# Constant fills and the first pair's products on VectorE, and the first batch's maximum of V twelve steps later, in a fused attention and two-layer feed-forward kernel

## The chip, the cores and the metric

The kernel runs on one core of a Trainium2 chip. The metric is the device time of one launch in microseconds (us); lower is better. Three runs of the kernel before took 1356.93, 1356.93 and 1362.55 us, so its median is 1356.93 us. PE is TensorE (matmuls), PEld its weight loads, DVE is VectorE, ACT is ScalarE, POOL is GpSimd, and SP is the engine whose queue issues all DMAs here.

## What is computed

The inputs are 4 batches of 12 heads, 448 rows and 64 columns. Attention is followed by a gated feed-forward layer and a second one with a cosine:

```python
q_n, k_n = rmsnorm(q, g_q), rmsnorm(k, g_k)
scores = scale * np.matmul(q_n, k_n.transpose(0, 1, 3, 2))
attn = softmax(scores)                       # rows, with their maximum taken off
x = np.matmul(attn, v)                       # heads are put side by side: 1792 x 768
g = x @ moe_w_gate
x = (g / (1 + exp(-g)) * (x @ moe_w_val)) @ moe_w_out
h = x @ moe2_w_in
out = (h * np.cos(h)) @ moe2_w_out
```

## The kernel before

**Pairs.** Two heads form a pair, so each batch has six pairs; those of batch 0 are numbered 0 to 5 here. Numbers are carried as a high and a low half in float16, so that most matmuls come in threes.

**Stages.** First the six pairs of batch 0 go through attention alone. Then the feed-forward pieces of batch b run (`mm_piece`, L1002 to L1004), with the attention of batch b+1 between them, and then the second layer. The weights are 64-bit-wide in memory: each load (768 KB, L821) is turned into 32-bit words by three DVE instructions (L841 to L843, one conversion), squared by ACT for a scale (L861), and split.

**A pair of batch 0**, in the order of its data:

- `p_load` loads its q and k (L281, L284), `c_v` its V in five DMAs (L606 to L609).
- `p_sq` squares (ACT, L311) and sums (DVE, L312); `p_pow` raises to the power -1/2 on POOL (L321) and, on DVE, multiplies k by the gains (L325).
- `p_mul` multiplies k (DVE, L363) and q (POOL, L364) by that root. `p_khi` and `p_qhi` copy the high halves (ACT, L378, L392), and `p_klo` and `p_qlo` subtract them to leave the low halves (POOL, L384, L398). Which engine does which is said by sets of letters, one set for each batch (`CF`, read by `cfg`): "qm", "kl" and "ql" put q's product and the two low halves on POOL.
- `c_T` transposes the halves by a DMA (L614) into a tile T. T has three buffers in this stage, so the transposition of pair 3 waits until pair 0's last matmul on T is done, that of pair 4 for pair 1, that of pair 5 for pair 2.
- `c_copy` moves parts of T (DVE L621 and L622, ACT L623). `c_s` makes seven score tiles only for their maxima (PE L634, DVE L635).
- `c_row` turns the maxima into a row (DVE L641 and L642, PE L646, ACT L647). `c_st` makes the transposed scores with that row taken off (PE L664) and their exponentials (ACT L667).
- `c_av` multiplies by V (PE L677), into two PSUM banks t and u that have one buffer each. `c_x` divides by the sums (ACT L683 and L684, DVE L685, a reciprocal, and two results at L690), using `vs2`. Only then are t and u free for the next pair.

**The maximum of V.** V is scaled by a power of two from the largest magnitude in its batch. `v_max(b)` loads V of the batch in two halves into the raw buffers that the weights also use (L333, 672 KB each), reduces each on DVE (L334), joins the partitions by a matmul (L337), makes the scales with five small DVE instructions (L339 to L343), and spreads them by a second matmul (L346) and a copy (L347). For batch 0 it also makes `vs2` (L349), which `c_x` needs.

**Constants.** `c_const(i)` fills, for each of three buffers C, the lower 64 partitions with zeros (L587) and two single rows with -2^14 (L589), and fills two other tiles, all on POOL.

**What sets the order.** The program emits steps n = -32 to 52 for batch 0 (`LEAD` is 33). In each step it emits pieces of several pairs. `v_max(0)` is emitted ahead of step `VM0 - LEAD`, `v_max(1)` after step `VM1` = 2. A scheduling layer then puts each engine's instructions in a fixed order, by its own estimate of times. On the chip each engine works through its own list strictly in that order, and SP its DMAs: an instruction that waits holds up everything behind it.

The raw buffers are three, taken in turn. The PSUM banks of the first feed-forward matmuls are those that `c_av` and `c_st` used, so that L1002 starts when `c_x` of pair 5 has read them.

Of the kernel before, what the change touches and what calls it, by code (L numbers as in the profile page):

```python
# [24 lines left out]
FD = 1  # L25
FH = 1
YS = (3, 2)
VM0 = 22
VM1 = 2
CAV = 1  # L30
CXX = 8
# [9 lines left out]
         26: [("split", 1), ("conv", 3), ("load", 5)]}  # L41
UNITS = ((0, 2, 4, 5), (0, 2, 4, 6), (0, 2, 4, 6), (0, 2, 4, 6))
SCH = ((1, 0), (0, 0), (1, 1))
OFF = ({'load': -25,
  'vload': -18,
  'sqk': -17,
# [94 lines left out]
def kernel(ctx: ExitStack, tc, q, k, v, g_q, g_k, w_gate, w_val, w_out, w2_in, w2_out, out):  # L141
    nc = tc.nc
# [12 lines left out]
    HP = P // 2  # L155
# [116 lines left out]
        return src[b, 2 * p:2 * p + 2].rearrange("h (q t) d -> (h q) t d", t=NS)  # L272

    def cfg(g):
        return CFS[g // NP]

    def p_load(g):
# [9 lines left out]
    def p_vload(g):  # L287
        rv = pool("rv", g).tile([P, 2, NS, D], F32, tag="rv", name="rv")
        b, p = divmod(g, NP)
        vs = v[b, 2 * p:2 * p + 2].rearrange("h (q t) d -> q h (t d)", t=NS)  # L290
        rv2 = rv.rearrange("p h t d -> p h (t d)")
        nc.sync.dma_start(rv2[:HP], vs)
        nc.sync.dma_start(rv2[HP:, :, :S - D], vs[:, :, D:])
        if g < NP:
            pass
        elif "vw" in cfg(g):
            nc.vector.tensor_copy(rv[HP:, :, NS - 1], rv[:HP, :, 0])
        else:
            nc.sync.dma_start(rv2[HP:, :, S - D:], vs[:, :, :D])
        prep[g]["rv"] = rv  # L300

    def p_sq(g, j):
        pg = prep[g]
        if j == 1:
            pg["ss"] = pools["sm"].tile([P, 2 * NS], F32, tag="ss", name="ss")
        sq = pool("sq", g, 2 * g + j).tile([P, S], F32, tag="sq", name="sq")
        src = pg["rqk"][:, j].rearrange("p g d -> p (g d)")
        if ("sq", "sk")[j] in cfg(g):
            nc.gpsimd.tensor_tensor(sq, src, src, op=ALU.mult)
        else:  # L310
            nc.scalar.activation(sq, src, AF.Square)  # L311
        nc.vector.tensor_reduce(  # L312
            pg["ss"][:, NS * j:NS * j + NS], sq.rearrange("p (g d) -> p g d", d=D), axis=AX.X, op=ALU.add
        )

    def p_pow(g):
        pg = prep[g]
        ss = pg["ss"]
        nc.vector.tensor_scalar(ss, ss, 1.0 / (D * PQ * PQ), 1e-6 / (PQ * PQ), op0=ALU.mult, op1=ALU.add)  # L319
        ri = pools["sm"].tile([P, 2, NS], F32, tag="ri", name="ri")  # L320
        nc.gpsimd.tensor_tensor(ri.rearrange("p a b -> p (a b)"), ss, half[:, :2 * NS], op=ALU.pow)  # L321
        pg["ri"] = ri
        if "kf" in cfg(g):
            k3 = pg["rqk"][:, 1]
            nc.vector.tensor_tensor(k3, k3, gk.unsqueeze(1).to_broadcast([P, NS, D]), op=ALU.mult)  # L325

    def v_max(b):
        half_n = H * S * D // P // 2
        src = v[b].rearrange("h s d -> (h s d)").rearrange("(p x) -> p x", p=P)
        vm = nm_p.tile([P, 4], F32, tag="nm", name="vm")  # L330
        for i in range(2):
            t = rot("raw").tile([P, 6 * 256], I32, tag="raw", name="raw")
            nc.sync.dma_start(t[:, :half_n].bitcast(F32), src[:, i * half_n:(i + 1) * half_n])  # L333
            nc.vector.tensor_reduce(vm[:, i:i + 1], t[:, :half_n].bitcast(F32), axis=AX.X, op=ALU.max, apply_absolute_value=True)  # L334
        nc.vector.tensor_max(vm[:, 2:3], vm[:, 0:1], vm[:, 1:2])
        ps = bank(ps_s, "s")
        nc.tensor.matmul(ps[:1, :P], vm[:, 2:3], ident, start=True, stop=True)  # L337
        row = nm_p.tile([1, 4], F32, tag="nm", name="vrow")
        nc.vector.tensor_reduce(row[:, 0:1], ps[:1, :P], axis=AX.X, op=ALU.max)  # L339
        nc.vector.tensor_scalar(row[:, 1:2], row[:, 0:1], 1e-30, None, op0=ALU.max)  # L340
        nc.vector.tensor_scalar(row[:, 1:2].bitcast(I32), row[:, 1:2].bitcast(I32), 0x7F800000, None, op0=ALU.bitwise_and)
        nc.vector.reciprocal(row[:, 2:3], row[:, 1:2])
        nc.vector.tensor_scalar(row[:, 2:3], row[:, 2:3], PV, None, op0=ALU.mult)  # L343
        nc.vector.tensor_scalar(row[:, 3:4], row[:, 1:2], 1.0 / (2.0 * PV), None, op0=ALU.mult)
        ps = bank(ps_s, "s")
        nc.tensor.matmul(ps[:, :2], full[:1], row[:, 2:4], start=True, stop=True)  # L346
        nc.vector.tensor_copy(vsc[:, 2 * b:2 * b + 2], ps[:, :2])  # L347
        if b == 0:
            nc.vector.tensor_scalar(vs2, vsc[:, 0:1], 2.0, None, op0=ALU.mult)  # L349
# [231 lines left out]
    def ctile(nm, shape, dt, g=None):  # L581
        return c_p.tile(shape, dt, tag="c" + nm, name="c" + nm, bufs=COL[nm])

    def c_const(i):

        C = ctile("C", [P, NS, P], F16)
        nc.gpsimd.memset(C[HP:], 0.0)  # L587
        for r in (HP, HP + 32):
            nc.gpsimd.memset(C[r:r + 1], -(2.0 ** 14))  # L589
        W = ctile("w", [P, NS, HP], F16)  # L590
        nc.gpsimd.memset(W, 0.0)
        if i < 2:
            V = ctile("V", [P, 4, 2, P], F32)
            nc.gpsimd.memset(V[:, :, 0, HP:], 1.0)
            nc.gpsimd.memset(V[:, :, 1, :HP], 1.0)
            colv[i] = V
        colc[i] = (C, W)
# [122 lines left out]
    def ph(g):  # L720
        return PH[g if g < NP else NP - 1 + g // NP]

    LEAD = -min(OFF[ph(g)][nm] + NS * g - CSH for g in range(NP) for nm, f in PREP)

    def s_prep(n):
        for nm, f in PREP:
            for g in range(NPAIR):
                if NS * g + OFF[ph(g)][nm] - (CSH if g < NP else 0) == n:
                    if g < NP and nm in ("vhi", "vlo"):
# [448 lines left out]
    for i in range(3):  # L1178
        c_const(i)
    step(-LEAD, 0)  # L1180
    for n in range(1 - LEAD, NB + NTAIL):
        if n == VM0 - LEAD:
            v_max(0)
# [22 lines left out]
    for b in range(B):  # L1206
        sched = {}
        if b + 1 < B:
            nst = NB + NTAIL
            q0, q1 = SCH[b][0], per - SCH[b][1]  # L1210
            wt = [1 if q0 <= u < q1 else 0 for u in range(per)]
# [136 lines left out]
```

## Time and profile before

| | us |
|---|---|
| median of three runs | 1356.93 |
| the profiled execution's own time | 1358.27 |
| its span, first to last instruction | 1356.5 |
| PE busy | 1199.2 (88%) |
| DVE busy | 883.3 (65%) |
| ACT busy | 684.4 (50%) |
| POOL busy | 474.5 (35%) |
| first matmul on a tile T | 37.59 |
| first feed-forward matmul (L1002) | 158.36 |

The profiled execution spends 1.77 us outside its span, and is 1.34 us above the median. In the rows of the next section but one, a row of a timeline says when a group of instructions started, how long it took from its first start to its last end, engine, line, operation, what it writes and reads, the shape, how many were merged (x3), and in brackets how long the engine had stood idle ahead of it and what it waited for. Neighbouring instructions of an engine overlap a little: one reduction of 448 elements takes 0.61 us, but the next starts some 0.53 us after it.

### The profile page before, as it was taken

To read this page: it belongs to the slowest core of one execution; us is meant where nothing else is said; L and a number is where in the kernel's file an instruction comes from. 1 tells how busy PE (TensorE), PEld (TensorE's weight loads), DVE (VectorE), ACT (ScalarE), POOL (GpSimd) and SP (SyncE) were. 2 spreads that over 40 slices of the span, in tenths; PEclk is the share of its full clock that TensorE was granted. 3 is DMA by queue.
4 is the path that set the end of the run, shared out by engine and by line. 5 is a ranking of instruction groups with operands and counts; after the bars stand their busy time and mean duration, and the time that the engine had idled before them with its cause. 6 is when DMAs were issued, how large, how long until landed. Compare 5 with 4: busy or idle time off the path is not lost.

```text
span 1356.5 us, 18241 instructions
## 1 busy us (share of the span) xinstructions
PE 1199.2 (88%) x6454; PEld 676.3 (50%) x6454; DVE 883.3 (65%) x1556; ACT 684.4 (50%) x1318; POOL 474.5 (35%) x351
## 2 busy tenths in 40 slices
PE   0588787878799978999999998979998999999998
PEld 0233343334574435854458655955444555666665
DVE  7868968999967787647763399477889875100000
ACT  2567577775435556445664365456767776100000
POOL 8621335555733456623554013503323332000000
PEclk9889798788899999999999999989999999999999
DMA  7535559987999976789867688641113222633121
GB/s 239 142 82 143 175 149 241 242 215 216 244 327 276 219 170 157 194 231 203 187 131 191 217 305 292 233 160 48 47 47 129 82 82 70 212 110 100 58 88 41
DMA packets 255195, 227.02 MB, mean 167 GB/s; under 512 B 177280, under 2 KB 205952, under 8 KB 255104
## 3 DMA queue, kind: packets, MB, share of 16 engines
q1 hardware_dynamic: 255104, 225.86, 59.3%
q8 instruction: 50, 0.82, 0.3%
q14 instruction: 41, 0.34, 0.1%
HBM read 147.13 MB, written 38.77 MB: 137 GB/s over the span
## 4 chain that ended last, share of the span: by engine, by line
PE 45%; DVE 19%; DMA 6%; ACT 4%; issue 3%; POOL 1%; SPq 0%; DVEq 0%; ACTq 0%; POOLq 0%
PE mm L1002 9%; PE mm L1003 8%; PE mm L1004 8%; PE mm L1015 7%; PE s L1015 7%; DMA T<-h 3%; PE t L1015 2%; DVE w L842 2%; DVE w L843 2%; PE t L555 2%; DVE w L841 2%; DMA PT<-p 2%; DVE tmp L1140 1%; PE s L444 1%; DVE sm L453 1%
## 5 line engine op out<-in xcount | busy, mean ns | idle before, releaser
L1002 PE MATMUL mm<-xy,wp 128*128 128x448 f16 x960 | 347.4, 363 | 35.9 <-DVE tmp L1144 12.2
L1003 PE MATMUL mm<-xy,wp 128*128 128x448 f16 x960 | 347.9, 362 | 0.0
L1004 PE MATMUL mm<-xy,wp 128*128 128x448 f16 x960 | 342.7, 362 | 2.2 <-DVE wp L874 2.1
L1015 PEld LDWEIGHTS <-g 128*128 128x128 f16 x1344 | 131.5, 98 | 87.2
L1002 PEld LDWEIGHTS <-wp 128*128 128x128 f16 x960 | 97.9, 102 | 120.9 <-issue 25.9
L1003 PEld LDWEIGHTS <-wp 128*128 128x128 f16 x960 | 96.3, 100 | 108.9 <-issue 33.5
L1004 PEld LDWEIGHTS <-wp 128*128 128x128 f16 x960 | 94.9, 100 | 98.5 <-issue 10.3
L1149 POOL TENSOR_TENSOR g<-tmp,g 128x448 f16<-128x448 f32 x64 | 73.7, 1165 | 188.3 <-ACT g L1148 188.3
L496 POOL TENSOR_TENSOR p<-pr,p 128x448 f16<-128x448 f32 x72 | 89.9, 1252 | 140.9 <-ACT p L487 122.2
L943 POOL TENSOR_TENSOR wp<-w,wp 128x768 fp32r<-128x768 f32 x48 | 96.3, 2010 | 79.7 <-ACT wp L942 50.2
L463 ACT ACTIVATE pr<-s,sm,esc 128x448 f32<-128x448 f32 x126 | 90.2, 718 | 60.0 <-DVE sm L457 56.8
L1002 PE MATMUL mm<-g,wp 128*128 128x448 f32 x288 | 108.6, 378 | 0.0
L1003 PE MATMUL mm<-g,wp 128*128 128x448 f32 x288 | 107.2, 372 | 0.0
L1004 PE MATMUL mm<-g,wp 128*128 128x448 f32 x288 | 106.7, 371 | 0.2 <-POOL wp L943 0.2
L1050 POOL TENSOR_TENSOR g<-tmp,g 128x448 fp32r<-128x448 f32 x48 | 63.8, 1343 | 108.7 <-ACT g L1049 108.5
L1015 PE MATMUL s<-wp,g 128*128 128x384 f16 x576 | 100.1, 326 | 0.0
L1015 PE MATMUL mm<-wp,g 128*128 128x384 f16 x576 | 99.1, 326 | 0.0
L453 DVE TENSOR_REDUCE sm<-s 128x1 f32<-128x448 f32 x126 | 75.5, 615 | 20.2 <-PE s L444 19.9
L487 ACT ACTIVATE p<-pr 128x448 f16<-128x448 f32 x126 | 70.0, 570 | 28.1 <-DMA PT<-p 27.1
L321 POOL TENSOR_TENSOR ri<-ss,half 128x14 f32<-128x14 f32 x24 | 64.5, 2692 | 47.1 <-DVE ss L319 39.3
L1160 ACT ACTIVATE tmp<-mm,osc 128x384 f32<-128x384 f32 x8 | 4.7, 581 | 148.6 <-PE mm L1015 147.8
L842 DVE SCALAR_TENSOR_TENSOR w<-raw,w 128x768 int32<-128x768 int32 x68 | 76.6, 1138 | 0.8
(170 smaller groups left out, 2078.0 us busy)
## 6 DMA issues: line engine op xcount, KB each, us to landing
raw<-in_moe_w_out_dram SPq DMA_DIRECT2D x28, 768.0 KB, 5.2
wp<-scr_gate SPq DMA_DIRECT2D x36, 384.0 KB, 4.4
wp<-scr_val SPq DMA_DIRECT2D x36, 384.0 KB, 4.7
w<-scr_out SPq DMA_DIRECT2D x36, 384.0 KB, 4.0
raw<-in_moe_w_in_dram SPq DMA_DIRECT2D x16, 768.0 KB, 4.7
raw<-in_moe_w_gate_dram SPq DMA_DIRECT2D x12, 768.0 KB, 5.5
raw<-in_moe_w_val_dram SPq DMA_DIRECT2D x12, 768.0 KB, 5.0
wp<-scr_out SPq DMA_DIRECT2D x24, 384.0 KB, 3.0
```

Source lines behind the costliest of these rows:

```text
L321: nc.gpsimd.tensor_tensor(ri.rearrange("p a b -> p (a b)"), ss, half[:, :2 * NS], op=ALU.pow)
L453: nc.vector.tensor_reduce(sm[:, 0, t:t + 1], slot[n][:, :S], axis=AX.X, op=ALU.max)
L463: nc.scalar.activation(e, slot.pop(n)[:, :S], AF.Exp, bias=sm[:, 1, t:t + 1], scale=esc, accum_out=sm[:, 2, t:t + 1],)
L487: nc.scalar.activation(hi, slot[n], AF.Copy)
L496: eng.tensor_sub(p16[:, t - t0, 1], slot.pop(n), p16[:, t - t0, 0])
L842: nc.vector.scalar_tensor_tensor(wi, hi, -0x40000000, wi, op0=ALU.bitwise_and, op1=ALU.bitwise_or)
L943: nc.gpsimd.tensor_sub(wl, w32, wh.bitcast(F32))
L1002: nc.tensor.matmul(ps[f][:, :S], wh[:, s], x[:, 0], start=(first and i == 0), stop=False)
L1003: nc.tensor.matmul(ps[f][:, :S], wh[:, s], x[:, 1], start=False, stop=False)
L1004: nc.tensor.matmul(ps[f][:, :S], wl[:, s], x[:, 0], start=False, stop=(last and i == n - 1))
L1015: nc.tensor.matmul(ps[:, :CO], x[:, a, p0:p0 + P], rhs, start=st, stop=sp)
L1149: nc.gpsimd.tensor_sub(x[:, 1], r, x[:, 0])
```

## The change

Three things are changed. `VM0` goes from 22 to 34, so that `v_max(0)` is emitted ahead of step 1 in place of step -11, just ahead of `v_max(1)`. The fills of C (three of zeros, six single rows) go from POOL to DVE. Pair 0 gets a set of its own, without "qm", "kl" and "ql": `p_mul` then multiplies q and k in one DVE instruction (L369 of the changed kernel), and both low halves are DVE subtractions. "kf" and "xl" stay as they were.

```diff
-VM0 = 22
+VM0 = 34
...
+FIRST = {'kf', 'xl'}
...
     def cfg(g):
+        if g == 0:
+            return FIRST
         return CFS[g // NP]
...
-        nc.gpsimd.memset(C[HP:], 0.0)
+        nc.vector.memset(C[HP:], 0.0)
         for r in (HP, HP + 32):
-            nc.gpsimd.memset(C[r:r + 1], -(2.0 ** 14))
+            nc.vector.memset(C[r:r + 1], -(2.0 ** 14))
```

Lines of the changed kernel are one higher from L44 on and three higher from L277 on. Three places in the engines' lists follow.

DVE around pair 0's product (rqk_285 and h16_312 or h16_313 are pair 0's, vm_357 and vm_470 are `v_max(0)`'s), before:

```order
L334 TENSOR_REDUCE vm_357<-raw_358 128x1
L334 TENSOR_REDUCE vm_357<-raw_361 128x1
L335 TENSOR_TENSOR vm_357<-vm_357 128x1
L339 TENSOR_REDUCE vrow_367<-s_365 1x1
L363 TENSOR_TENSOR rqk_285<-rqk_285,ri_308 128x448
L340 TENSOR_SCALAR vrow_367<-vrow_367 1x1
L341 TENSOR_SCALAR vrow_367<-vrow_367 1x1
L342 RECIPROCAL vrow_367<-vrow_367 1x1
```

and of the change:

```order
L337 TENSOR_REDUCE vm_470<-raw_471 128x1
L322 TENSOR_SCALAR ss_337<-ss_337 128x14
L369 TENSOR_TENSOR rqk_285<-rqk_285,ri_308 128x896
L337 TENSOR_REDUCE vm_470<-raw_474 128x1
L366 TENSOR_TENSOR rqk_303<-rqk_303,ri_329 128x448
L387 TENSOR_TENSOR h16_312<-rqk_285,h16_312 128x7x64
L401 TENSOR_TENSOR h16_312<-rqk_285,h16_312 128x7x64
L338 TENSOR_TENSOR vm_470<-vm_470 128x1
L366 TENSOR_TENSOR rqk_323<-rqk_323,ri_357 128x448
L844 TENSOR_SCALAR w32_735<-raw_579 128x768
```

Pair 0's product has moved ahead of the second half's reduction, and the low halves stand behind that reduction.

SP's list at the first loads of V (raw tiles are for the maximum, cV_267 is pair 0's V and cV_276 pair 1's), before:

```order
L284 DMA rqk_324<-in_q_dram 128x448
L333 DMA raw_358<-in_v_dram 128x1344
L333 DMA raw_361<-in_v_dram 128x1344
L606 DMA cV_267<-in_v_dram 64x4x64
...
L609 DMA cV_267<-in_v_dram 64x64
L606 DMA cV_276<-in_v_dram 64x4x64
```

and of the change:

```order
L287 DMA rqk_323<-in_q_dram 128x448
L609 DMA cV_267<-in_v_dram 64x4x64
...
L612 DMA cV_267<-in_v_dram 64x64
L336 DMA raw_471<-in_v_dram 128x1344
L336 DMA raw_474<-in_v_dram 128x1344
L609 DMA cV_276<-in_v_dram 64x4x64
```

The two halves for the maximum now stand behind the five loads of pair 0's V.

DVE between the rows of pair 0 (cw_265) and of pair 1 (cw_274), before:

```order
L641 TENSOR_SCALAR cw_265<-sm_386 128x7
...
L363 TENSOR_TENSOR rqk_521<-rqk_521,ri_694 128x448
L319 TENSOR_SCALAR ss_1081<-ss_1081 128x14
L339 TENSOR_REDUCE vrow_540<-s_538 1x1
...
L347 COPY vsc_101<-s_547 128x2
L635 TENSOR_REDUCE sm_448<-s_555 128x1
L635 TENSOR_REDUCE sm_574<-s_575 128x1
L641 TENSOR_SCALAR cw_274<-sm_448 128x7
```

and of the change (vm_529 is `v_max(1)`'s, vrow_480 `v_max(0)`'s and vrow_539 `v_max(1)`'s, w32_810 and w32_885 are the second and third conversion, T_663 is pair 3's, cr_644 pair 0's sums):

```order
L644 TENSOR_SCALAR cw_265<-sm_364 128x7
...
L337 TENSOR_REDUCE vm_529<-raw_530 128x1
L337 TENSOR_REDUCE vm_529<-raw_533 128x1
...
L844 TENSOR_SCALAR w32_810<-raw_581 128x768
...
L844 TENSOR_SCALAR w32_885<-raw_583 128x768
...
L624 COPY cB_679<-T_663 64x896
...
L688 RECIPROCAL cr_644<-cr_644 128x448
L343 TENSOR_SCALAR vrow_539<-vrow_539 1x1
L693 SCALAR_TENSOR_TENSOR tmp_649<-t_512,vs2_102,cr_644 64x448
...
L350 COPY vsc_101<-s_546 128x2
L638 TENSOR_REDUCE sm_426<-s_554 128x1
...
L644 TENSOR_SCALAR cw_274<-sm_426 128x7
```

Between the two rows now also stand the two reductions of `v_max(1)`, two weight conversions, pair 3's `c_copy` and pair 0's `c_x`; before, those reductions and conversions stood ahead of pair 0's first score maximum, and the `c_copy` and `c_x` behind pair 1's row.

## Rows read from the trace of the kernel before

**Rows 1.** Windows: stretch, length, PE, PEld, DVE, ACT, POOL busy, PEclk, DMA share, GB/s.

```profile
0.00:22.80 22.80, 1.17 (x4) 0.61 (x4) 12.89 (x35) 5.21 (x8) 21.36 (x34) 1.00 0.59 187
...
61.20:147.80 86.60, 73.72 (x285) 28.34 (x285) 66.66 (x107) 57.20 (x104) 18.36 (x14) 0.90 0.46 119
147.80:158.40 10.60, 1.16 (x9) 0.84 (x6) 10.52 (x13) 5.42 (x14) 7.96 (x5) 0.61 0.50 126
```

**Rows 2.** Timeline of the first 28 us, all engines.

```profile
1.27 0.84 POOL L587 MEMSET cC<- 64x896 f16 x1
...
7.37 0.90 SPq L333 DMA_DIRECT2D raw<-in_v_dram  x2
...
10.15 3.50 POOL L589 MEMSET cC<- 1x896 f16 x4
...
12.28 0.62 SPq L609 DMA_DIRECT2D cV<-in_v_dram  x1
...
13.74 7.72 POOL L321 TENSOR_TENSOR ri<-ss,half 128x14 f32<-128x14 f32 x3
...
16.70 1.55 DVE L334 TENSOR_REDUCE vm<-raw 128x1 f32<-128x1344 f32 x1 [1.02 <-DMA raw<-in_v_dram]
...
19.43 0.60 DVE L363 TENSOR_TENSOR rqk<-rqk,ri 128x448 f32<-128x448 f32 x1
...
21.57 1.27 DVE L363 TENSOR_TENSOR rqk<-rqk,ri 128x448 f32<-128x448 f32 x1
...
27.90 3.36 SPq L614 DMA_TRANSPOSE T<-h  x1
```

**Rows 3.** The raw tiles of the first 60 us: from issue to landing.

```profile
DMA to landing us min/median/max: 4.1/6.1/8.8
```

**Rows 4.** The transpositions of L614: from issue to landing.

```profile
DMA to landing us min/median/max: 4.0/4.2/6.2
```

**Rows 5.** Timeline of DVE from 22 to 76 us.

```profile
22.80 3.21 DVE L334 TENSOR_REDUCE vm<-raw 128x1 f32<-128x1344 f32 x2
...
30.97 0.55 DVE L841 TENSOR_SCALAR w<-raw 128x768 int32<-128x768 int32 x1
...
33.43 0.55 DVE L841 TENSOR_SCALAR w<-raw 128x768 int32<-128x768 int32 x1
...
36.42 1.11 DVE L622 COPY T<-T 64x896 f16<-64x896 f16 x1
...
49.88 0.17 DVE L641 TENSOR_SCALAR cw<-sm 128x7 f16<-128x7 f32 x1
...
61.15 0.94 DVE L641 TENSOR_SCALAR cw<-sm 128x7 f16<-128x7 f32 x1
...
66.97 0.39 DVE L621 COPY cB<-T 64x896 f16<-64x896 f16 x1 [1.75 <-DMA T<-h]
...
70.02 2.95 DVE L685 RECIPROCAL cr<-cr 128x448 f32<-128x448 f32 x1 [0.27 <-ACT cr L684]
...
75.12 0.69 DVE L690 SCALAR_TENSOR_TENSOR tmp<-u,vs,cr 64x448 f32<-64x448 f32 x1
```

**Rows 6.** Timeline of PE from 65 to 159 us.

```profile
65.45 0.41 PE L646 MATMUL s<-id,cw 128*64 128x128 f16 x4
...
68.49 0.58 PE L634 MATMUL s<-T 128*64 128x448 f16 x2 [2.27 <-DVE sm L635]
...
71.54 1.30 PE L664 MATMUL c<-cB,cC 128*128 128x448 f16 x3
...
93.93 3.47 PE L677 MATMUL t<-pr,cV 128*128 128x448 f32 x8
...
158.36 0.56 PE L1002 MATMUL mm<-xy,wp 128*128 128x448 f16 x1 [5.22 <-DVE tmp L690]
```

**Rows 7.** Timeline of SP's queue: the transpositions of pairs 3 and 4.

```profile
61.53 2.16 SPq L614 DMA_TRANSPOSE T<-h  x1
...
76.08 1.55 SPq L614 DMA_TRANSPOSE T<-h  x1
```

## The prediction

> **What bounds the kernel now.** I read the windows by stage first, because the change touches only the first stage, then the timeline of each engine there. Up to 22.8 us nothing is bound by work: DVE is busy for 12.89 us, PE for 1.17, and POOL for 21.36 [rows 1]. The reader should see POOL's queue in it: six row fills end at 13.65, and only then the three roots start, at 13.74 [rows 2]. DVE meanwhile stands at the second half of V, which lands at 16.70, and pair 0's product waits behind it until 19.43 [rows 2]. Its first transposition goes out at 27.90 [rows 2], and DVE has both copies done at 36.42 + 1.11 = 37.5 [rows 5]. From there on it is a chain of pairs: PE is busy for 73.7 of 86.6 us between 61.2 and 147.8, DVE for 66.7 [rows 1]. Neither is full; two loops tie them. Transpositions 3 and 4 go out when `c_st` of pairs 0 and 1 is done, at 61.53 and 76.08 [rows 7], and pair g+1 may multiply by V only when `c_x` of pair g has emptied t and u. The stage ends on DVE: busy for 10.52 of the last 10.6 us [rows 1], and L1002 starts when the last result of `c_x` is out, at 158.36 [rows 6].
>
> **Fills.** POOL loses 3 x 0.84 + 6 x 0.87 = 7.7 us [rows 2]. Its first root then starts when the sums are there, 2 to 3 us before 13.74. On DVE nothing of before shows such a fill. The bounds are nothing and POOL's own price, 7.7 us; I take the latter, the only row of the same shape. Five of nine stand ahead of the gains' arithmetic, where DVE waits for a load; four behind it cost 3.4 us, before the sums. DVE has 9.9 idle us in this window [rows 1], so either end is hidden. The Trainium skill, page "VectorE: DVE Perf Modes", section "Zero memsets can be issued as uint32 (trn2)", gives one cycle for each element of a fill whatever its type; by that the nine would take an estimated 7.0 us, and no run here shows it.
>
> **The head start.** Pair 0's product no longer waits for the V maximum's small instructions, but its low halves stand behind the reduction of V's second half, and V's halves now stand behind five loads of pair 0's V. Those take SP from 8.27 to 12.90, so the halves go out 4.6 us later, at 12 to 12.8 [rows 2]. Landing takes 4.1 to 8.8 us [rows 3]; the middle, 6.1, puts the second half at 18.9. Behind it stand its reduction, 1.55, and three operations at some 0.53 each (DVE's step between such instructions), so 22 to 22.5; with one hand-over from ACT I take 23, between 21 and 25. That is 4.9 us ahead of 27.90. The transposition lands 4.0 to 6.2 us later [rows 4]; I take 5.8, near the longest, since a weight load goes out just ahead of it. DVE has two instructions of that load's conversion ahead of `c_copy` and one within it, and is done at some 31.4, not 37.5. **Head start: 6.1 us.** Up to pair 0's row DVE's list then has the same instructions as before, 49.88 - 37.5 = 12.4 us [rows 5], so that the row comes at 43.8.
>
> **What it is paid with.** Between the rows of pairs 0 and 1 passed 61.15 - 49.88 = 11.3 us [rows 5]. Now the list has there as well: the two reductions of V of batch 1, 3.2; two conversions, each 33.43 - 30.97 = 2.46; pair 0's `c_x`, a reciprocal of 2.95 and two results of 0.7; and pair 3's two copies, 0.8 [rows 5]. Together 13.3 us. The second conversion's load can go out only when the first of the reductions has freed its buffer, near 50.5, and lands 4.1 us later at the least [rows 3], when DVE has been there for a microsecond; I add 1.5. Pair 1's row is then at 43.8 + 11.3 + 13.3 + 1.5 = 70, not 61.15. These are instructions that DVE did before under the wait for the first transposition; that cover is gone, and PE is queued behind them, since the second matmul of `v_max(1)` stands ahead of pair 1's last scores and waits for DVE's list to have passed pair 0's results.
>
> **How much comes back.** Before, PE had pair 1's row at 65.45 but began its `c_st` at 71.54, having waited for pair 3's copies (2.27 us of wait at 68.49) [rows 6], because transposition 3 went out at 61.53 and its copy began at 66.97 [rows 5, 7]. Now transposition 3 goes out near 54, when pair 0's `c_st` is done, and its copies lie in the list above. So PE goes from the row to `c_st` in some 3.6 us, at 73.6: 2.1 later than before. That `c_st` took 76.08 - 71.54 = 4.5 us [rows 6, 7]. Now four of pair 1's products with V stand within it, at 3.47 / 4 = 0.87 each [rows 6], and two more score tiles: some 9 us, and transposition 4 at 82.6, 6.5 late. From it to pair 2's products with V passed 93.93 - 76.08 = 17.9 us [rows 6, 7], half a pair's products (3.5) of which are done already: 97.0 in place of 93.93. **Net: 3 us late.** From there PE's list is the same as before up to L1002, and takes the same 64.4 us [rows 6]. DVE is full in the last 10.6 us [rows 1], so some of the lateness may vanish in PE's wait there; I leave it at 3, with nothing and 6.5 (transposition 4's own lateness) as ends. Where batch 1 lies between the feed-forward pieces, the lists differ in places until about a third of PE's instructions are through, and not after. I count nothing for it, and 4 us either way for the range, about what one displaced transposition costs [rows 4].
>
> **A rule against the change.** Pair 0's DVE product and subtractions, which read two tiles, now run beside POOL's roots. A DVE product took 0.60 us beside the roots at 19.43 and 1.27 beside a POOL product at 21.57 [rows 2]: the roots did not hold it, the product did. The Trainium skill, page "SBUF — State Buffer", section "The single rule", says that a DVE instruction with two SBUF inputs and a GpSimd instruction that reads SBUF exclude each other for a whole instruction. By that rule a root too could hold DVE; the trace agrees for the POOL product and not for the roots.
>
> **The sum.** The profiled execution took 1358.27 us; plus 3 is 1361.3. It lies 1.34 above the median of the three runs, so on the median's scale 1356.9 + 3 = 1360.
>
> **Rivals.**
> (1) The head start is kept. For it: in the 86.6 us of pairs DVE has 20 idle us [rows 1], and `c_x` of pair 0, done at 75.8 before [rows 5], is now done near 67, so t and u are free when pair 1 wants them. Against it: one list, in order. It decides by pair 1's row: ahead of 66 us, PE reaches pair 1's `c_st` ahead of 71.5 and the chain keeps 4 to 6 us. At 6.1 us the time is 1351. Chance 0.26.
> (2) The loop doesn't close again: products of pair 1 that are placed within `c_st` wait for their exponentials, so nothing of a pair's products is saved, and the 17.9 us count in full. Pair 2's come at 82.6 + 17.9 = 100.5, 6.5 late; with the bound for the later lists 1360 to 1367, middle 1363.5 to 1364. It decides from a fourth transposition later than 82 us. Slower than before. Chance 0.20.
> (3) The head start fails: pair 0's DVE instructions wait for a root of 7.72 / 3 = 2.6 us [rows 2]. Transposition 0 at 25.6 and everything 2.6 later than forecast: 1362.6. Chance 0.06; this is what the rule above would do, by the trace's own price.
> The forecast has the rest, 0.48.
>
> **Range and chances.** 0.5% is 6.8 us, about what a measurement of this kernel can tell from no change: 1350.1 to 1363.7. From the forecast, 1360 with 4 us either way, some 0.06 lies above; from rival 1 half lies below, and 0.03 of the forecast's and other tails; from rival 2 some 0.13 above; from rival 3 0.02. Faster 0.16, slower 0.21, same 0.63. For 8 in 10 the range must reach rival 1's time and all of rival 2's: 1350 to 1368.
>
> **What would show it.** POOL's first root ahead of 12 us; transposition 0 issued near 23, pair 0's first score maximum near 32, its row near 44: the head start. Pair 1's row near 70, PE idle for some 10 us ahead of it with the wait on DVE, transposition 4 near 82.6: the payment. Pair 2's products with V near 97 and L1002 near 161.4: the net. The prediction is wrong in its mechanism if pair 1's row comes ahead of 66 us, or if L1002 starts more than 7 us from 158.4; and wrong about the rest if L1002 moves by 3 us and the end by far more.

## The result, and the profile after

The change is slower. Its four runs took 1372.63, 1376.95, 1378.31 and 1378.36 us, median 1377.63, beside 1359.34 for the kernel before on the same chip: ratio 1.012, 95% interval 1.0099 to 1.0141. The forecast was 1360.0 with a range of 1350 to 1368, so the time lies 9.6 us above the range. The profiled execution of the change took 1372.63 us (span 1370.8), 14.4 more than that of before.

Windows of the change (columns as in [rows 1]):

```profile
0.00:22.80 22.80, 0.00 (x0) 0.00 (x0) 18.92 (x38) 6.55 (x11) 15.46 (x26) 1.00 0.76 209
61.20:147.80 86.60, 65.91 (x268) 26.23 (x269) 66.77 (x110) 55.80 (x100) 15.60 (x11) 0.88 0.40 107
147.80:158.40 10.60, 3.54 (x14) 1.52 (x12) 10.57 (x12) 7.60 (x18) 3.65 (x3) 0.82 0.68 188
```

Against [rows 1], DVE is busy for 18.92 in place of 12.89 us of the first window and POOL for 15.46 in place of 21.36. DVE still has idle time there; whether the fills were covered is tested in E3. In the stretch of pairs PE is busy for 65.9 in place of 73.7 us. Timeline of the change's first stage (several engines):

```profile
1.03 1.38 DVE L590 MEMSET cC<- 64x448 uint32 x3
...
6.12 0.81 DVE L592 MEMSET cC<- 1x896 f16 x1 [0.24 <-DVE gk L236]
...
11.48 6.55 POOL L324 TENSOR_TENSOR ri<-ss,half 128x14 f32<-128x14 f32 x2 [6.46 <-DVE ss L322]
...
17.04 1.09 DVE L369 TENSOR_TENSOR rqk<-rqk,ri 128x896 f32<-128x896 f32 x1
...
18.04 1.55 DVE L337 TENSOR_REDUCE vm<-raw 128x1 f32<-128x1344 f32 x1
...
21.34 4.54 SPq L617 DMA_TRANSPOSE T<-h  x1
...
44.06 0.17 DVE L644 TENSOR_SCALAR cw<-sm 128x7 f16<-128x7 f32 x1
...
70.74 0.56 PE L349 MATMUL s<-vrow,full 1*128 1x2 f32 x2 [11.81 <-DVE vrow L346]
...
72.93 0.17 DVE L644 TENSOR_SCALAR cw<-sm 128x7 f16<-128x7 f32 x1
...
85.31 1.57 SPq L617 DMA_TRANSPOSE T<-h  x1
...
98.64 3.47 PE L680 MATMUL t<-pr,cV 128*128 128x448 f32 x8 [1.38 <-DVE tmp L693]
...
161.07 0.55 PE L1005 MATMUL mm<-xy,wp 128*128 128x448 f16 x1 [4.53 <-DVE tmp L693]
```

The head start is there: transposition 0 at 21.34 (27.90 in [rows 2]), pair 0's row at 44.06 (49.88 in [rows 5]). So is the payment: PE stands for 11.81 us at the second matmul of `v_max(1)`, pair 1's row comes at 72.93 (61.15), the fourth transposition at 85.31 (76.08 in [rows 7]). Then most of it comes back, and the first feed-forward matmul starts at 161.07, 2.7 us later than in [rows 6]. Everything else, 11.7 us, is lost where the prediction counted nothing.

**Where it is lost.** The table follows one matmul line, L1007 (L1004 before), which runs once for every three feed-forward matmuls, by the start of its 1st, 193rd, 385th, 481st and 601st matmul. Kernel before in us from the span's start, all others as delay against it. E1 to E12 are the experiments below, the time is that of the profiled execution.

| | 1st | 193rd | 385th | 481st | 601st | its time | median of runs | ratio, 95% |
|---|---|---|---|---|---|---|---|---|
| before | 159.1 | 382.7 | 550.9 | 623.2 | 723.4 | 1358.27 | | |
| the change | +2.7 | +2.0 | +5.1 | +12.9 | +14.3 | 1372.63 | 1377.6 | 1.0120 (1.0099 to 1.0141) |
| E1 VM0 = 33 | +4.7 | +2.8 | +2.6 | +1.9 | +2.2 | 1360.84 | 1360.4 | 1.0003 (0.9985 to 1.0020) |
| E2 VM1 = 3 | +8.3 | +7.2 | +6.9 | +6.3 | +8.3 | 1365.77 | 1363.5 | 1.0026 (1.0007 to 1.0046) |
| E3 fills back on POOL | +3.6 | +2.8 | +8.3 | +16.6 | +18.4 | 1377.03 | 1377.0 | 1.0119 (1.0088 to 1.0149) |
| E5 fills alone | +1.1 | -0.2 | +0.4 | +3.9 | +3.6 | 1362.31 | 1366.6 | 1.0051 (1.0034 to 1.0068) |
| E6 fills and VM0 | +3.3 | +5.5 | +5.3 | +8.3 | +7.4 | 1367.86 | 1368.8 | 1.0074 (1.0052 to 1.0095) |
| E7 pair 0's set alone | -5.1 | -5.7 | -3.1 | -4.0 | -2.2 | 1356.28 | 1354.9 | 0.9969 (0.9954 to 0.9984) |
| E8 VM0 alone | +7.4 | +5.4 | +6.4 | +9.0 | +9.0 | 1367.44 | 1364.9 | 1.0046 (1.0027 to 1.0065) |
| E9 batch 3 loaded earlier | +3.5 | +1.8 | +8.2 | +7.6 | +8.7 | 1366.51 | 1370.8 | 1.0079 (1.0052 to 1.0106) |
| E10 batch 3 multiplied later | +5.1 | +5.9 | +8.0 | +11.5 | +13.6 | 1372.03 | 1372.5 | 1.0083 (1.0060 to 1.0106) |
| E11 batch 2 loaded earlier | +4.2 | +3.8 | +7.0 | +9.2 | +10.8 | 1368.09 | 1365.4 | 1.0041 (1.0025 to 1.0058) |
| E12 set alone, VM0 = 24 | +8.7 | +6.1 | +6.1 | +5.0 | +6.3 | 1364.73 | 1362.2 | 1.0026 (1.0010 to 1.0041) |

(E4 has no row: its profiled execution took 1768.98 us at a mean granted clock of 0.66, and it is left out of medians and ratios, as is one of E9's of 4190.53 us.) From the 385th to the 481st the change takes 80.1 us and before 72.3. That is the end of batch 2's attention. In batches 1 to 3 the probabilities of a pair get high halves on ACT (L490 of the change) and low halves on DVE or POOL (L499), go through a transposition by DMA (L509) and are then multiplied by V on PE (L558); before, each of these lines is three lower. Until the last pair's are there, PE fills the time with feed-forward matmuls. PE, and the engines ahead of it, before (L283 loads k of batch 3's next pair, L444 makes the pair's last scores, L453 takes their maxima):

```profile
535.27 0.34 SPq L283 DMA_DIRECT2D rqk<-in_k_dram  x1
...
545.86 0.38 PE L444 MATMUL s<-T 128*64 128x448 f16 x2
...
546.48 1.16 DVE L453 TENSOR_REDUCE sm<-s 128x1 f32<-128x448 f32 x2
...
548.39 1.92 DVE L366 TENSOR_TENSOR rqk<-rqk,ri 128x896 f32<-128x896 f32 x1 [0.64 <-POOL ri L321]
...
552.42 2.26 DVE L496 TENSOR_TENSOR p<-pr,p 128x448 f16<-128x448 f32 x1
...
556.61 2.04 DVE L496 TENSOR_TENSOR p<-pr,p 128x448 f16<-128x448 f32 x1
...
558.85 0.37 PE L1004 MATMUL mm<-g,wp 128*128 128x448 f32 x1
561.68 1.51 PE L555 MATMUL t<-PT,vh 128*64 128x448 f16 x14 [2.46 <-DMA PT<-p]
563.00 1.07 PE L555 MATMUL t<-PT,vl 128*64 128x448 f16 x8
```

and in the change:

```profile
545.36 1.67 SPq L509 DMA_TRANSPOSE PT<-p  x1
547.12 1.06 SPq L286 DMA_DIRECT2D rqk<-in_k_dram  x1
...
550.96 0.38 PE L447 MATMUL s<-T 128*64 128x448 f16 x2
...
556.28 1.15 DVE L456 TENSOR_REDUCE sm<-s 128x1 f32<-128x448 f32 x2
...
559.07 1.92 DVE L369 TENSOR_TENSOR rqk<-rqk,ri 128x896 f32<-128x896 f32 x1 [1.39 <-POOL ri L324]
...
559.22 1.04 ACT L490 ACTIVATE p<-pr 128x448 f16<-128x448 f32 x2
...
560.01 4.88 POOL L946 TENSOR_TENSOR wp<-w,wp 128x768 fp32r<-128x768 f32 x2
...
561.02 2.15 DVE L376 TENSOR_TENSOR rqk<-rqk,gk 128x448 f32<-128x448 f32 x1
563.10 1.82 DVE L515 TENSOR_SCALAR sm<-sm 128x7 f32<-128x7 f32 x1
...
565.18 0.94 DVE L416 COPY W<-T 64x896 f16<-64x896 f16 x1
566.16 2.16 DVE L499 TENSOR_TENSOR p<-pr,p 128x448 f16<-128x448 f32 x1
...
568.77 0.62 DVE L499 TENSOR_TENSOR p<-pr,p 128x448 f16<-128x448 f32 x1
...
573.41 2.83 PE L558 MATMUL t<-PT,vh 128*64 128x448 f16 x14 [8.08 <-DMA PT<-p]
576.03 1.84 PE L558 MATMUL t<-PT,vl 128*64 128x448 f16 x8
```

The reader should see three things. The high halves of the last probabilities (ACT L490) are there at 560.3, but DVE subtracts them (L499) only at 566.2 and 568.8, since the next pair's product, its gains, the sums and a copy stand ahead in its list. PE has then run out of other work and waits 8.08 us, not 2.46. And its 22 matmuls take 4.4 us in place of 2.3.

Product and gains stood ahead of the subtractions before as well, so they are not what is new. DVE was late already when it came to the maxima of the last scores: 5.3 us after PE began these scores, where it was 0.6 before. From these maxima to the end of the last subtraction then passed 13.1 us, and 12.2 before. So 4.7 us of the delay lie ahead of the maxima and 0.9 behind them. From the last subtraction to PE's matmul passed 4.0 us in place of 3.0, and five more feed-forward matmuls cover 1.0 of the sum: 5.6 us are left as wait. What made DVE late by the maxima is not pinned to one instruction. A sign of it is on SP: the next pair's k goes out behind a transposition of probabilities (L509), 3.8 us ahead of the last scores in place of 10.6, and DVE sums the squares of that pair just ahead of the maxima (554.25 and 555.56), where it had these sums done at 541.5 before. E9 below loads the pair earlier.

The windows show why the matmuls took longer; the change's wait and those matmuls:

```profile
565.30:573.40 8.10, 0.04 (x1) 0.00 (x0) 4.54 (x5) 1.51 (x2) 4.18 (x3) 0.64 0.69 137
573.40:577.80 4.40, 4.39 (x22) 1.78 (x23) 0.69 (x1) 0.00 (x0) 0.00 (x0) 0.50 0.85 254
```

and the same matmuls before:

```profile
561.70:564.00 2.30, 2.30 (x22) 1.35 (x22) 0.69 (x1) 0.00 (x0) 0.00 (x0) 1.00 0.86 291
```

The granted clock fell to 0.50 (1.2 GHz) during the idle time, and was 1.00 (2.4 GHz) before. The sum, 8.08 - 2.46 + 4.4 - 2.3 = 7.7 us, is the stretch's loss of 7.8.

### The profile page after: what moved, and what is told of

Its sections match the earlier page's. It is cut to its first block, busy times and chain, and to the rows that moved or that the text cites. A ratio compares the mean times of both kernels' runs of the same rounds, so it can differ in the third digit from the quotient of the medians.

```text
span 1370.8 us, 18242 instructions
## 1 busy us (share of the span) xinstructions
PE 1195.4 (87%) x6454; PEld 672.2 (49%) x6454; DVE 887.9 (65%) x1567; ACT 683.4 (50%) x1318; POOL 465.4 (34%) x339
## 4 chain that ended last, share of the span: by engine, by line
PE 39%; DVE 14%; ACT 4%; DMA 3%; issue 2%; SPq 1%; POOL 0%; DVEq 0%; ACTq 0%; POOLq 0%
PE mm L1005 7%; PE mm L1007 7%; PE mm L1006 7%; PE s L1018 7%; PE mm L1018 7%; PE t L1018 2%; DVE tmp L1143 1%; DVE w L846 1%; PE t L558 1%; DVE w L845 1%; DVE tmp L1144 1%; DVE tmp L1147 1%; ACT tmp L1146 1%; DMA PT<-p 1%; DVE w L844 1%
## 5 line engine op out<-in xcount | busy, mean ns | idle before, releaser
L1005 PE MATMUL mm<-xy,wp 128*128 128x448 f16 x960 | 346.2, 362 | 38.0 <-DVE tmp L1042 13.0
L1007 PE MATMUL mm<-xy,wp 128*128 128x448 f16 x960 | 341.8, 360 | 1.1 <-DVE wp L877 1.0
L1005 PEld LDWEIGHTS <-wp 128*128 128x128 f16 x960 | 97.7, 102 | 120.1 <-issue 24.7
L1007 PEld LDWEIGHTS <-wp 128*128 128x128 f16 x960 | 94.9, 100 | 96.7 <-issue 9.6
L499 POOL TENSOR_TENSOR p<-pr,p 128x448 f16<-128x448 f32 x72 | 87.5, 1219 | 127.2 <-ACT p L490 110.6
L946 POOL TENSOR_TENSOR wp<-w,wp 128x768 fp32r<-128x768 f32 x48 | 99.6, 2079 | 72.9 <-ACT wp L945 45.9
L1007 PE MATMUL mm<-g,wp 128*128 128x448 f32 x288 | 106.0, 369 | 3.5 <-POOL wp L946 3.5
L1005 PE MATMUL mm<-g,wp 128*128 128x448 f32 x288 | 107.0, 372 | 0.0
L1006 PE MATMUL mm<-g,wp 128*128 128x448 f32 x288 | 106.0, 368 | 0.0
L490 ACT ACTIVATE p<-pr 128x448 f16<-128x448 f32 x126 | 69.9, 570 | 18.3 <-DMA PT<-p 17.2
```

The source lines that it names most:

```text
L490: nc.scalar.activation(hi, slot[n], AF.Copy)
L499: eng.tensor_sub(p16[:, t - t0, 1], slot.pop(n), p16[:, t - t0, 0])
L946: nc.gpsimd.tensor_sub(wl, w32, wh.bitcast(F32))
L1005: nc.tensor.matmul(ps[f][:, :S], wh[:, s], x[:, 0], start=(first and i == 0), stop=False)
L1006: nc.tensor.matmul(ps[f][:, :S], wh[:, s], x[:, 1], start=False, stop=False)
L1007: nc.tensor.matmul(ps[f][:, :S], wl[:, s], x[:, 0], start=False, stop=(last and i == n - 1))
```

## The experiments

Two theories. **O**: the first stage costs some 3 us, as forecast, and the rest comes from the order in which the lists stand behind it. **S**: the late start costs the rest by itself, since everything then meets its loads and buffers at other moments.

**E1, E2: nearly the same first stage, the later lists of before.**

```diff
-VM0 = 34
+VM0 = 33
```

> The change with VM0 = 33 in place of 34; fills and pair 0's set as in the change. SP's list is that of the change through the whole first stage, DVE's differs in the place of some 13 instructions around pair 0's maxima; from shortly after the first feed-forward matmul every engine's list is that of the kernel before, where the change's lists differ up to about a third of PE's instructions. Theory O (the order: of the 14.4 us, 2.7 are the first stage's, as forecast, and the rest are lost where the lists between the feed-forward pieces differ): first L1005 at 159 to 163 us, PE's wait for the transposed probabilities near 562 to 566 us at 2 to 3.5 us as before and not 8.1, the time 1358 to 1363 us, ratio 1.000 to 1.004. Rival S (the late start costs the rest by itself, because everything after it meets its loads and buffers at other moments): 1368 to 1374 us, ratio 1.008 to 1.013, with the delay growing between 400 and 700 us.

```diff
-VM1 = 2
+VM1 = 3
```

> The change with VM1 = 3 in place of 2, so that the maximum of V of batch 1 is emitted one step later. Through the first stage the lists are those of the change but for some ten small DVE instructions, which put pair 1's row ahead of five of them; after it the lists are those of the kernel before. Theory O: first L1005 at 159 to 162, time 1357 to 1362 us, ratio 0.999 to 1.004. Rival S: as the change, 1368 to 1374, ratio 1.008 to 1.013.

Measured: E1 1.0003 and E2 1.0026. They start the feed-forward 4.7 and 8.3 us late, later than the change does, and end 2 and 8 us late: nothing grows (table). One step of one emission constant takes the loss away. The wait in E1:

```profile
563.34 1.51 PE L558 MATMUL t<-PT,vh 128*64 128x448 f16 x14 [1.54 <-DMA PT<-p]
```

S falls. E2's first matmul was later than I had expected (L1005 at 166.7 against 159 to 162), and so was its end (median 1363.5 against 1357 to 1362).

**E3: the fills.**

```diff
-        nc.vector.memset(C[HP:], 0.0)
+        nc.gpsimd.memset(C[HP:], 0.0)
         for r in (HP, HP + 32):
-            nc.vector.memset(C[r:r + 1], -(2.0 ** 14))
+            nc.gpsimd.memset(C[r:r + 1], -(2.0 ** 14))
```

> The change with the nine fills put back on GpSimd. PE's list is word for word that of the change in the whole program, and so are the other engines' lists behind the first 37 instructions. Theory O: it pays what the change pays, ratio 1.009 to 1.014, with the wait of some 8 us for the transposed probabilities near 570 us; the first transposition comes at 21.3 to 24 us, since the second half of V (18.0 us in the change) and not the roots holds it. If the fills carried the loss (DVE's list or its port), it would come back here: ratio below 1.004.

Measured: 1.0119, the change's own time, and with the change's list of PE its wait too:

```profile
576.63 2.82 PE L558 MATMUL t<-PT,vh 128*64 128x448 f16 x14 [8.13 <-DMA PT<-p]
```

Which engine does the fills is worth nothing in this change. Transposition 0 goes out at 20.07, 1.3 us ahead of the change's and a little earlier than expected, but pair 0's row comes at 45.10, 1.0 behind it.

**E4 to E8: the parts**, each as an edit of the change. E4, fills and set:

```diff
-VM0 = 34
+VM0 = 22
```

> Fills on VectorE and pair 0's own set, but VM0 left at 22, so that both maxima of V and two conversions stand ahead of pair 0's first maxima as before. Lists after the first stage differ from before's only up to a seventh of PE's instructions. Theory O with the payment as forecast (the price of the head start is what VM0 puts between the rows of pairs 0 and 1): first transposition at 23 to 25.5 us, pair 1's row before 61, first L1005 at 154 to 157.5, time 1352 to 1357, ratio 0.996 to 1.000. Rival P (the payment comes with any head start, because DVE is behind by the same work): L1005 at 158 to 162, ratio 1.000 to 1.004.

Measured: 1356.0 us, ratio 0.9973 (0.9956 to 0.9989), as theory O has it. No row of its first stage is used, so this run does not decide between O and P there. E5, the fills alone:

```diff
-VM0 = 34
+VM0 = 22
...
         if g == 0:
-            return FIRST
+            return CFS[0]
```

> Only the nine fills go to VectorE; VM0 = 22 and pair 0's set as in the kernel before. In the first stage PE's list hardly moves; behind it the lists differ from before's as far as the change's do (up to about a third of PE's instructions), and in several places as the change's (the matmuls on the second and third pair's transposed probabilities of batch 1 stand behind 252 and 360 feed-forward matmuls, as in the change, not behind 288 and 324). Theory O (the later lists carry the loss): first L1005 at 157 to 161, and the lists cost 3 to 12 us behind it: 1361 to 1372, ratio 1.003 to 1.010. If fills cost nothing and the order costs nothing: 1356 to 1360, ratio within 0.002 of 1.

Measured: 1.0051. The first stage is 1.1 us late. In the trace 3.5 us are lost between the 385th and the 481st matmul, where PE waits 4.37 us for the last transposed probabilities: an edit that costs a microsecond where it stands costs several more by the order that it brings about. The trace shows 4.0 us in all; its execution was nearly the fastest of E5's, and the median lies 7.4 us above that of before, so some 3 us are seen in no trace. E6, fills and VM0:

```diff
         if g == 0:
-            return FIRST
+            return CFS[0]
```

> Fills on VectorE and VM0 = 34, without pair 0's own set (its product and low halves stay on GpSimd). PE's list is that of the change through the whole first stage, and SP's and ACT's too; behind it they differ from the change's and from before's: one group of scores early in the attention of batch 2 stands behind 828 feed-forward matmuls as in the kernel before, in the change behind 792, and the last pair's matmuls on transposed probabilities behind 1194 as before, in the change behind 1199. Theory O: first L1005 at 160 to 165 (the product on GpSimd starts the chain some 1 to 3 us later than in the change), and then whatever these lists cost: with the wait near 565 us gone, 1362 to 1369; with it, 1372 to 1378. Rival S (the late start itself): 1370 to 1378 whatever that wait does.

Measured: 1.0074. With the change's first stage and other later lists the wait is 2.84 us, and from the 385th to the 481st it takes 75.3 us, not 80.1. E7, the set alone:

```diff
-VM0 = 34
+VM0 = 22
...
-        nc.vector.memset(C[HP:], 0.0)
+        nc.gpsimd.memset(C[HP:], 0.0)
...
-            nc.vector.memset(C[r:r + 1], -(2.0 ** 14))
+            nc.gpsimd.memset(C[r:r + 1], -(2.0 ** 14))
```

> Only pair 0's own set; fills on GpSimd and VM0 = 22. Behind the first stage the lists are before's but for the first seventh of PE's instructions. Theory O with the payment as forecast (what VM0 puts between the rows of pairs 0 and 1 is the price): no payment, transposition 0 at 24 to 26.5 us in place of 27.9, first L1005 at 155 to 158, 1353 to 1357, ratio 0.997 to 1.000. Rival P (any head start is paid back between the rows): first L1005 at 158 to 161, ratio 1.000 to 1.003.

Measured: 0.9969 (0.9954 to 0.9984), the fastest kernel of the study. The fourth transposition, pair 1's row and PE's first feed-forward matmul:

```profile
56.11 3.73 SPq L617 DMA_TRANSPOSE T<-h  x1
...
60.74 0.92 DVE L644 TENSOR_SCALAR cw<-sm 128x7 f16<-128x7 f32 x1
...
153.22 0.55 PE L1005 MATMUL mm<-xy,wp 128*128 128x448 f16 x1 [6.18 <-DVE tmp L693]
```

L1005 starts 5.1 us earlier than in [rows 6], earlier than expected too (155 to 158), but not because nothing was paid between the rows: pair 0's row came at 41.97, 7.9 us ahead of before, and pair 1's at 60.74, only 0.4 ahead. So rival P is right about the rows and wrong about the end. What the rows lose comes back through the transposition of pair 3, which goes out at 56.11 in place of 61.53 [rows 7], and that of pair 4, at 70.30 in place of 76.08. Of the 5.1 us, some 3 are lost again behind (table). E8, VM0 alone:

```diff
-            return FIRST
+            return CFS[0]
...
-        nc.vector.memset(C[HP:], 0.0)
+        nc.gpsimd.memset(C[HP:], 0.0)
...
-            nc.vector.memset(C[r:r + 1], -(2.0 ** 14))
+            nc.gpsimd.memset(C[r:r + 1], -(2.0 ** 14))
```

> Only VM0 = 34; fills on GpSimd, pair 0's product and low halves on GpSimd as in the kernel before. Lists are before's from inside the first stage on. Theory O with the payment as forecast: transposition 0 at 23 to 26, pair 1's row at 70 to 75 as in the change, first L1005 at 160 to 166, nothing lost behind it: 1359 to 1365, ratio 1.001 to 1.006. If VM0 alone were harmless in the first stage: first L1005 before 158, ratio at or below 1.

Measured: 1.0046. Transposition 0 went out at 27.47 (expected 23 to 26), pair 1's row came at 72.47 us and the first matmul 7.4 us late; little is lost behind it. So the set gives 5.1, VM0 takes 7.4 and the fills 1.1: +3.4 together, beside the change's +2.7.

**E9 to E11: the change with one entry of `OFF` altered**, the table that says at which step each piece of a pair is emitted. The lists stay the change's up to a point; in E9 and E10 this lies some 30 to 65 us ahead of the wait.

```diff
- {'load': -16,
+ {'load': -17,
```

> The change, with one entry of the table of offsets altered: pairs of batch 3 are loaded one step earlier (-17 in place of -16). Every engine's list is that of the change up to about 512 us; from there to some 660 us it differs, and around the end of batch 2's attention it is close to the list of the kernel before (the last pair's two subtractions for the low halves of the probabilities stand on DVE right behind the next pair's product and gains, not behind sums, reciprocal and a copy as well; on ACT the next pair's squares stand ahead of the last exponentials' group as before). Theory D (the 8.1 us wait for the last transposed probabilities comes from what stands ahead of them on ACT and DVE in the change's list): that wait is 2 to 4.5 us, and the time is 6 to 9 us below the change's: 1368 to 1372, ratio 1.006 to 1.010. Rival S (it comes from how late everything is by then): the wait stays at 6.5 us or more, 1375 to 1379.

Measured: 1.0079, by the medians 6.8 us below the change. The two intervals still touch (1.0052 to 1.0106 and 1.0099 to 1.0141), so the trace has to carry the reading. k of the next pair is now loaded at 542.69, 11.4 us ahead of the last scores and ahead of the transposition of probabilities that it stood behind in the change, and DVE takes the last maxima 0.7 us after those scores began. One subtraction stands right behind the gains, the other ends at 565.6, and the wait is short:

```profile
560.84 2.26 DVE L499 TENSOR_TENSOR p<-pr,p 128x448 f16<-128x448 f32 x1
...
565.03 0.57 DVE L499 TENSOR_TENSOR p<-pr,p 128x448 f16<-128x448 f32 x1
...
568.93 1.52 PE L558 MATMUL t<-PT,vh 128*64 128x448 f16 x14 [1.46 <-DMA PT<-p]
```

The stretch takes 71.6 us. The profiled execution had lost 6.4 us between the 193rd and the 385th matmul, so that it ends only 6.1 us ahead of the change's.

```diff
-  'mul': -10,
+  'mul': -9,
```

> The change, with pairs of batch 3 multiplied by their roots one step later (-9 in place of -10). Lists are the change's up to about 543 us. At the end of batch 2's attention DVE then has the next pair's product behind both subtractions of the last probabilities, while ACT's list stays as in the change there (two squares of the next pair ahead of the last exponentials). If DVE's queue is what holds the last transposed probabilities: wait 2 to 5 us in place of 8.1, 1370 to 1374. If ACT's order holds them, by the exponentials being late: wait 6 us or more, 1374 to 1379.

Measured: 1.0083, by the medians 5.2 us below the change. DVE's list has the product (L369) behind both subtractions, while ACT still has the next pair's squares ahead of the last exponentials:

```profile
560.49 1.04 ACT L490 ACTIVATE p<-pr 128x448 f16<-128x448 f32 x2
...
564.96 2.79 DVE L499 TENSOR_TENSOR p<-pr,p 128x448 f16<-128x448 f32 x2
567.67 1.08 DVE L369 TENSOR_TENSOR rqk<-rqk,ri 128x896 f32<-128x896 f32 x1
...
572.38 1.51 PE L558 MATMUL t<-PT,vh 128*64 128x448 f16 x14 [3.77 <-issue]
```

PE stands for 3.77 us, and its matmuls stay at full speed (1.51). The stretch takes 75.7 us, 4.4 less than in the change: with ACT's order as it was, DVE's list carries that much of the 7.8. The product's place is not all of it: DVE also came to the last maxima sooner, 3.1 us after the scores in place of 5.3. With the lists of before the stretch takes 71.2 to 74.9 us (E1, E2, E7, E8, E12 and before itself), so whether the rest belongs to ACT's order is open.

```diff
-   {'load': -11,
+   {'load': -12,
```

> The change, with pairs of batch 2 loaded one step earlier (-12 in place of -11). Lists are the change's up to some 465 us and those of the kernel before from some 515 us on. Theory O: the first stage's 2.7 us and what is lost up to 515 us (0 to 4) remain, the wait at the end of batch 2's attention is 2 to 4.5 us as before: 1361 to 1368, ratio 1.001 to 1.006. Rival S: 1372 or more.

Measured: 1.0041, 12 us below the change's median. With before's lists from some 515 us on, the wait is 2.96 us. What its profiled execution loses between the 193rd and the 385th matmul (3.2 us) the change loses too (3.1).

**E12: the set alone, with VM0 = 24.**

```diff
-VM0 = 34
+VM0 = 24
...
-        nc.vector.memset(C[HP:], 0.0)
+        nc.gpsimd.memset(C[HP:], 0.0)
...
-            nc.vector.memset(C[r:r + 1], -(2.0 ** 14))
+            nc.gpsimd.memset(C[r:r + 1], -(2.0 ** 14))
```

> Pair 0's own set with VM0 = 24, fills on GpSimd. From inside the first stage on all lists are those of the kernel before, where those of the set alone (VM0 = 22) differ up to a sixth of PE's instructions. If the set's gain in the first stage (some 5 us at the first feed-forward matmul) is kept, and its loss behind it came from the lists: 1351 to 1355, ratio 0.994 to 0.998. If the maximum of V two steps later already costs as at 34: first feed-forward matmul at 158 or later, ratio 1.000 or more.

Measured: 1.0026, with the first feed-forward matmul at 167.01: the set's gain is gone, as the second of the two cases has it. DVE's rows show where:

```profile
32.92 2.99 DVE L337 TENSOR_REDUCE vm<-raw 128x1 f32<-128x1344 f32 x2
...
44.55 0.56 DVE L844 TENSOR_SCALAR w<-raw 128x768 int32<-128x768 int32 x1 [0.17 <-DMA raw<-in_moe_w_gate_dram]
...
54.23 0.47 DVE L644 TENSOR_SCALAR cw<-sm 128x7 f16<-128x7 f32 x1
```

Two steps put both reductions of `v_max(1)` and two conversions in among pair 0's maxima, so that its row comes at 54.23 (41.97 in E7). Beside the set, two steps cost 13.8 us at the first L1007 (+8.7 in place of -5.1); twelve steps by themselves cost 7.4 (E8). Here what displaced work costs depends on which row it lands ahead of, not on how far it was moved.

## Why the prediction was right, and where it was wrong

- **Fills**: right. The nine rows add up to 3 x 0.43 + 6 x 0.81 = 6.1 us on DVE; counted from start to start (0.48 and 1.03 us, with DVE standing 0.22 us between the single rows) they take 7.6. Either is within the bounds of nothing and 7.7, and is covered by pair 0's row; E3 shows it. The page "VectorE: DVE Perf Modes" of the Trainium skill, section "Zero memsets can be issued as uint32 (trn2)", gave an estimated 7.0 us, which lies between the two counts: the trace agrees with it to that extent.
- **Head start**: right. Said 23, between 21 and 25, for transposition 0 and 43.8 for pair 0's row; 21.34 and 44.06. That the row agrees within 0.3 us is in part luck: the five loads of V took SP 3.3 us and not 4.6, so that V's halves went out from 10.44 and not from 12, and DVE's copies were done at 30.5 in place of 31.4; from there to the row passed 13.6 us in place of 12.4. The product beside a root took 1.09 us for two tiles (0.60 for one in [rows 2]), so rival 3 does not happen.
- **Payment**: right in kind, 3 us small. Pair 1's row was to come at 70 and came at 72.93; between the rows passed 28.9 us where the sum had 26.1. By the prediction's own sign it decides rival 1: later than 66, nothing kept. E7 shows that this sign is weaker than the prediction took it to be: there the row had kept 0.4 us, and the end of the stage 5.1.
- **What comes back**: right in kind, and the match at the end is in part luck. Transposition 4 went out at 85.31 (said 82.6), pair 2's products with V came at 98.64 (said 97.0), the first feed-forward matmul at 161.07 (said 161.4): 1.6 us late at the products, and 62.4 us from there in place of 64.4. Rival 2's condition held (a fourth transposition later than 82) but not its price: pair 2's products were not at 100.5, and from transposition 4 to them passed 13.3 us, not 17.9. In the four other runs with PE's list of the change in the first stage (E3 and E9 to E11) the first L1007 came 3.6, 3.5, 5.1 and 4.2 us late, so that "net 3" is the low end of what this stage does.
- **The later lists**: wrong, and this is the step that failed: "I count nothing for it, and 4 us either way for the range, about what one displaced transposition costs". It cost 11.7 us. The count of nothing took "the lists differ" for noise around zero. But the order of before is one that others fall back to (E1, E2, E8 and E12 rejoin it near the first feed-forward matmul or ahead of it), and the change's is a different one, worse in a definite place. The bound was wrong in kind: the price of a displaced transposition is not its landing time, but how long PE is left without matmuls, 5.6 us more, and what the clock then takes, 2.1. A bound from rows would have had to look for the places in the later stage where PE already waited (2.46 us at L555) and ask what stands ahead of the last scores' maxima and of the last subtraction in the new list.
- The last sentence on what would show it, "wrong about the rest if L1002 moves by 3 us and the end by far more", is what happened.

**What stays open.** The change's 3.1 us between the 193rd and the 385th matmul and 1.4 behind the 481st are measured, but no run here pins them to an instruction. The change's profiled execution was also its fastest; its median is 5 us above. E3, with the same list of PE, was profiled near its median and shows where most of the rest goes: it ends 4.4 us later than the change's, 2.4 of them lost between the 193rd and the 385th matmul (5.5 in place of 3.1). Why the same list costs more in one execution than in another stays open.

## What to carry to other kernels

Where a scheduling layer orders the whole program, an edit at its start can move instructions hundreds of microseconds later: compare the lists to their end, and price the differences where an engine runs out of covering work. Before such an edit is judged, run it with a neighbouring constant (a step more or less): if the time jumps by more than the edit can be worth, it is the order that was measured. And take a change of three parts apart: here one part gained 0.3% (E7) and kept it beside the fills (E4), and VM0 hid it, by its first stage (E8) and, together with the set, by the later order (E3). The parts do not simply add up: the fills cost 0.5% alone (E5), nothing beside the set (E4) and nothing in the whole change (E3).

## What was not expected of the hardware

- A subtraction, a small scale and a copy on DVE were stretched beside products on POOL: L515, 128x7, took 1.82 us beside L946 in place of 0.17, the copy L416 0.94 beside L401 in place of 0.39 (E1), and L499 2.16 beside L946 in place of 0.62. Before, the subtractions were stretched as much (2.26 and 2.04), so of these only L515 is new at this place. The Trainium skill, page "SBUF — State Buffer", section "Who interferes with whom" with its single rule, has them: two-input DVE instructions contend with GpSimd's reads, and so can a tensor_scalar or a copy. The trace agrees with it here.
- PE's granted clock was 0.50 after 8.1 us without work, and the matmuls after it took almost twice as long (2.83 for 1.51). After waits of 2.46 and 3.77 us the first matmuls were at full speed (1.51 in before and E10); in E11, after 2.96 us, they took 2.40, and in E8, after 3.23 us, 2.70. In these runs the length of the wait alone does not tell it.
